# A fused convolution and SiLU block: 25 weight sums spread over GpSimd's queue, and one block's halo moved ahead of another's stores

## The chip, the cores and the metric

The kernel runs on one core of a Trainium2 chip. The metric is the device time of one execution in microseconds (us). Before the change it is 2310.44 us, the median of three runs (2310.09 to 2311.41).

The engines are named TensorE (PE in the profile, its weight loads PEld), VectorE (DVE), ScalarE (ACT), GpSimd (POOL) and SyncE (SP). Each runs its own instructions in the order of the program and waits at semaphores for the others. SyncE does nothing but issue DMAs; GpSimd issues the DMAs that add to their destination.

## The reference

```python
# x: (8, 4096, 192), weight: (8 heads, 7 taps), w_in: (192, 2048), w_out: (2048, 192)
w = exp(weight - max(weight)); w = w / (sum(w) + 1e-9)      # per head
x_pad = concat(zeros(6 rows), x)                            # along the sequence
y[b, s, h, :] = sum_k w[h, k] * x_pad[b, s + k, h, :]       # 24 channels per head
h = y.reshape(32768, 192) @ w_in
out = (h * sigmoid(h)) @ w_out
```

So each token's 192 channels are first replaced by a weighted sum over seven tokens, and then go through two matrix products with a SiLU between them.

## The kernel before

**Tiling.** The 32768 tokens are taken in 32 blocks of 1024 (`TT`), and a block is held as two halves of 512 on the two halves of the 128 partitions. The 192 channels are three groups of 64. The hidden layer's 2048 columns are 16 chunks of 128.

**A block's stages.** `ld` loads the block into the tile `nat` by SyncE (L167). `i.2`, `i.1`, `i.0` are VectorE transposes of its three channel groups into `xt` (`turn_in`, L502). `xt` is one tile for all blocks, and a block has one of two `nat` tiles. `ha.0` (`halo_in`, L514) puts the six tokens before each half into the head of `xt`: for the first half a copy of a saved tail (by ScalarE for the blocks up to the fourth, L521), for the second half a DMA from the first half's end by SyncE (L524). `v.ki` is tap `i` of channel group `k` (`conv`, L530). Its first tap is a ScalarE product that writes into `nat` (L539). From the third block's group 2 on, each later tap is a ScalarE product into a buffer called `u` (L542) and a DMA of GpSimd that adds this to `nat` (L543); before that, VectorE adds the taps (L547). `sp` copies the result into the tile `dup` by SyncE (L569) and `w` makes differences of it on VectorE (`win`).

**The products.** Both matrix products are done with fewer multiplications, in the manner of Strassen: 15 products `P` for each of five groups of blocks of `w_in` (`P5.1` is product 5 of group 1, L681), three plain ones `L`, and 20 products `Q` for each quarter of `w_out` (L817). The results of the `P` products are combined on ScalarE and VectorE: a token `u4.1` is a ScalarE copy of a partial result into a `u` buffer (L730), `X`, `a` and `b` are VectorE sums (L724), `S` and `SL` the SiLU on ScalarE (L742, L747). There are ten `u` buffers for these copies and for the taps together. They are a list from whose front a buffer is taken and to whose end it is returned, in the order of the program; a tap's buffer goes back to the list at once, so that its next user has to wait for the tap's DMA. Sums of the SiLU's results are `tA1` (GpSimd), `tB1`, `tC`, `tD` and `t5` to `t13` (VectorE, all L806).

**The weights' own sums.** The products need sums of weight blocks, and GpSimd makes them in place, once: for `w_in` in `combine` (the `late` ones of these in steps `go`), for `w_out` in `combine_out` (L449), which runs through the 25 sums of `OUT_SUMS`, each of 128x256 numbers into `wall` or `wx` (recorded at L149, the helper that pins the order). The first block does its second product without those sums (`down_plain`, L889, steps `dp`) from the plain `w_out`, so that the 25 sums must come behind its last reading of `wall`, and ahead of the second block's `Q` products.

**The order.** Everything stands in an order written out by hand. `START` (L106) holds the steps from the first block to the second, `PLAN` (L80) one pass that is run again for each later block, `FINISH` the end. A sign ahead of a token tells whose it is: none is the pass's own block, `-` the block before, `=` the one before that, `+` the next one. `step` (L939) does a token once; what `START` has done, the passes leave out. `START` is read as of the third block, so that `+i.2` in it is of the fourth, `-P5.4` of the second and `=dp.0` of the first. Before the change, all 25 sums are emitted inside the last `dp` step of `START`. The fourth block's `i.1` stands at the end of the pass in which the second block's own products begin, and its `i.2`, `i.0` and `ha.0` at the beginning of the next, thus behind `=stp.0 =stp.1 =stp.2`, the twelve stores of the first block (L930), which wait for its output transposes `op` on VectorE (L921) and the copies `cp` on ScalarE (L913).

In the pass that is changed, the second block's products run in this order (the first twelve are `P5.4 P5.0 P2.4 P2.0 P3.4 P6.4 P6.0 P3.0 P1.0 P1.4 P13.4 P9.4`), with some of the steps of other engines between them:

```text
P5.1 u0.0 P13.0 P0.0 S2.4 u0.4 +v.20 P0.4 P9.0 P12.4 X4.4 u5.1 S2.0 P11.4 u1.4 P2.1 P7.4
... +v.10 ... P4.4 b5.4 a1.4 S3.0 +v.11 P3.1 ... P5.2 S0.4 S2.1 P10.0 P2.3 u5.2 u4.3 +v.00
... tA1 P7.1 ... P12.3 P0.3 +v.12 P9.2 a5.3 tC2 P0.2 P13.2 P4.3 S4.3 +v.24 ... P8.2 Q4.3 ...
```

Of the kernel before, what the change touches and what calls it, by code (L numbers as in the profile page):

```python
# [17 lines left out]
def kernel(  # L18
# [33 lines left out]
    NK = D // R  # L52
# [7 lines left out]
    NJ = NM // 2  # L60
# [56 lines left out]
    )  # L117
    FINISH = (
# [22 lines left out]
    def pin(ins):  # L141
        return tc.keep_in_program_order(ins)
# [110 lines left out]
    def load_in(j, queue, ks=None):  # L253

        if ("i", j) not in raws:
            raw_tile(("i", j))
        raw = raws["i", j].rearrange(AS[j], a=2, k=NK)
        for e in range(2) if ks is None else ():
            for a in range(2):
                queue.dma_start(  # L260
                    out=raw[R * e : R * e + R, a, :, :], in_=in32[:, :, a, 2 * j + e, :]
                )
        for k in ks or ():
            for e in range(2):
                queue.dma_start(
                    out=raw[R * e : R * e + R, :, k, :], in_=in32[:, k, :, 2 * j + e, :]
                )
# [77 lines left out]
    def comb(out, u, v, op):  # L345
        pool.tensor_tensor(out, u, v, op=op)
# [3 lines left out]
    def raw(g, i, k, e):  # L350
        a, j, own = chunks(g)[i]
        return rows(wr[j] if own == e else ws[j], e)[:, a, k, :]

    def combine(g, e):
# [38 lines left out]
    OUT_SUMS = (  # L393
        (("o", 7), ("o", 4), "+", ("o", 7)),
        (("x", 0), ("o", 1), "+", ("o", 7)),
        (("o", 1), ("o", 1), "+", ("o", 4)),
        (("o", 4), ("o", 4), "+", ("o", 10)),
        (("x", 1), ("o", 11), "+", ("o", 4)),
        (("o", 4), ("o", 4), "n", ("o", 4)),
        (("x", 2), ("o", 5), "+", ("x", 1)),  # L400
        (("x", 1), ("o", 8), "-", ("x", 1)),
# [41 lines left out]
    def out_form(at):  # L443
        if at[0] == "x":
            return wx[:, at[1], :, :]
        k, third = divmod(at[1], NK)
        return wall[:, :, k // 2, k % 2, R * third : R * third + R]

    def combine_out():  # L449
        for to, u, sign, v in OUT_SUMS:  # L450
            u = zeros[:, 0:R].unsqueeze(1).to_broadcast([P, NJ, R]) if sign == "n" else out_form(u)
            comb(out_form(to), u, out_form(v), ALU.add if sign == "+" else ALU.subtract)

    load_in(0, nc.sync, (0,))

# [149 lines left out]
    def rows(t, e):  # L605
        return t[R * e : R * e + R]
# [48 lines left out]
    def chain_bank(b, g, c):  # L655
        return banks[CHAIN_BANKS[c][g]]

    def x_bank(b, g, o):
        return banks[XBANKS[o][g]]
# [4 lines left out]
    def columns(half):  # L664
        return slice(0, TB) if half is None else slice(half * TB // 2, (half + 1) * TB // 2)

    def product(b, g, r, half=None):
        cols = columns(half)
        e = int(r in ON_B and (g, r) != SWAP)
        if r in RIGHT:  # L670
            rhs = rows(wins[b], e)[:, RIGHT[r], :]
        else:
            rhs = rows(dups[b], e)[:, SLOT[e][X_OF[r]], :]
        if r in (13, 11):
            to, first = x_bank(b, g, 2 if r == 13 else 4), False
        else:
            c = next(c for c in range(3) if r in CHAINS[c])
            to, first = chain_bank(b, g, c), r == CHAINS[c][0] and (b, g, c) not in begun
            begun.add((b, g, c))
        pin(  # L680
            nc.tensor.matmul(  # L681
                to[:, cols],
                raw(g, *LEFT[e][r], e),
                rhs[:, cols],
                start=first,
                stop=True,
                skip_group_check=True,
            )
        )
# [101 lines left out]
    def g_part(name, js):  # L791
        kind, i = name[0], int(name[1:])
        if kind == "s":
            return g_part(G_SUMS[i][3], js)
        if kind == "t":
            return temps[i][:, js, :]
        k, n = divmod(i, 2)
        at = TB * (2 * n + k % 2)
        return gall[:, js, k // 2, at : at + TB]
# [8 lines left out]
    def out_bank(node):  # L808
        name, e = OUT_HOME[node]
        return rows(banks[OUT_BANKS[name]], e)  # L810

    def out_product(b, r, j):
        node = next(x for x in OUT_ORDER if r in OUT_ORDER[x])
        first = node in ("X", "Y", "O4") and (b, node) not in begun
        begun.add((b, node))
        pin(
            nc.tensor.matmul(  # L817
                out_bank(node),
                out_form(OUT_FORMS[r])[:, j, :],
                g_part(OPERAND[r], j),  # L820
                start=first,
                stop=True,
                skip_group_check=True,
            )
        )
# [46 lines left out]
    def turn_out(b, i):  # L872
        pin(nc.vector.transpose(mid(2 + i), mid(i - 1)))  # L873
# [15 lines left out]
    def down_plain(b):  # L889

        cmbs[b] = [xpool.tile([P, 4, TB], F32, tag="cmb", name="cmb")]
        for j in range(NJ):
            for a in range(2):
                for e in range(2):
                    for k in range(NK):
                        for n in range(2):
                            pin(
                                nc.tensor.matmul(  # L898
                                    banks[DOWN_BANKS[k]][R * n : R * n + R, :],
                                    wo[j][:, a, e, R * k : R * k + R],  # L900
                                    g_tile(b, j, a)[:, n, e, :],
                                    start=j == 0 and a == 0 and e == 0,
                                    stop=j == NJ - 1 and a == 1 and e == 1,
                                    skip_group_check=True,
                                )
                            )
                        if (a, e, k) == (1, 1, NK - 1):
                            if j == NJ - 1:
                                combine_out()
                        yield  # L910

    def copy_plain(b, k):
# [26 lines left out]
    def step(b, token):  # L939

        if token[0] in BACK:
            b, token = b - BACK[token[0]], token[1:]
        name, _, arg = token.partition(".")
        if b < 0 or b >= NB or (b, token) in did:
            return
        did.add((b, token))
        digits = [int(c) for c in arg] if arg.isdigit() else []
        if name[0] == "P":
            product(b, digits[0], int(name[1:]))
        elif name == "L":  # L950
            plain(b, *digits)
        elif name == "SL":
            silu_plain(b, *digits)
        elif name[0] in "uXabS":
            sums_h(b, name, *digits)
        elif name[0] == "Q":
            out_product(b, int(name[1:]), *digits)
        elif name[:2] == "tA":
            sum_g(b, int(name[2:]), slice(0, NJ - 1), nc.gpsimd)
        elif name[:2] == "tB":  # L960
            sum_g(b, int(name[2:]), slice(NJ - 1, NJ), nc.vector)
        elif name[:2] in ("tC", "tD"):
            i = NJ // 2 if name[1] == "D" else 0
            sum_g(b, int(name[2:]), slice(i, i + NJ // 2), nc.vector)
        elif name[0] == "t":
            sum_g(b, int(name[1:]), slice(0, NJ), nc.vector)
        elif name in ("O", "C", "d"):
            out_copy(b, token)
        elif name == "m":
            out_sum(b, *digits)  # L970
        elif name == "o":
            turn_out(b, *digits)
        elif name == "st":
            store_out(b, *digits)
        elif name == "dp":
            next(downs)
        elif name == "cp":
            copy_plain(b, *digits)
        elif name == "op":
            turn_plain(b, *digits)  # L980
        elif name == "stp":
            store_plain(b, *digits)
        elif name == "go":
            some(late, digits[0])
        elif name == "ld":
            load(b, digits)
        else:
            {"i": turn_in, "ha": halo_in, "v": conv, "sp": spread, "w": win}[name](
                b, *digits
            )  # L990
# [62 lines left out]
    def some(ups, n):  # L1053
        for _ in range(n):
            next(ups, None)
# [71 lines left out]
```

## Time and profile before

| | us |
|---|---|
| median of three runs | 2310.44 |
| lowest and highest | 2310.09, 2311.41 |
| the profiled execution | 2310.77 |
| its span, first to last instruction | 2309.1 |
| idle before ScalarE's `u` copies (L730), whole span | 125.2 |
| GpSimd busy | 655.7 |
| one pass of 1024 tokens, for example from 225.07 to 295.42 | 70.35 |

The mean granted clock of TensorE is 0.998 of full speed over the span.

How to read what follows: times are from the span's start. A row of a timeline has start, duration, engine, line, operation, what it writes and reads, and in brackets how long the engine was idle before it and what ended that. A row of the waits has who waited for whom, the total, how many times, and the longest. A row of a line has the shortest, median and longest duration in ns. "To landing" is the time from a DMA's issue until its semaphore tells of its completion.

### The profile page before, as it was taken

Reading aid. Unit: us, or ns where it says so; the run is one execution under the profiler, and the core shown is the slowest. Engines: PE = TensorE matmul, PEld = TensorE weight load, DVE = VectorE, ACT = ScalarE, POOL = GpSimd, SP = SyncE. Lnnn points to the kernel's source line nnn. Section 1 sums busy time; section 2 is a strip of 40 time slices with the busy share of each in tenths; the row PEclk is TensorE's granted clock in tenths of the full one; section 3 lists DMA queues with packets and bytes.
Section 4 is the critical chain, followed back from the end, with each engine's and each line's share of the span. In section 5 each row is a group of like instructions: output and inputs, shape, how many; then the busy total and the mean of one; then the engine's idle time right before and its main releaser. Section 6 shows DMA issues by size and latency. Waiting matters only on the chain.

```text
span 2309.1 us, 31726 instructions
## 1 busy us (share of the span) xinstructions
PE 2290.7 (99%) x10622; PEld 926.5 (40%) x10622; DVE 2004.6 (87%) x2265; ACT 1554.1 (67%) x2842; POOL 655.7 (28%) x734
## 2 busy tenths in 40 slices
PE   9989999999999999999999999999999999999998
PEld 4334333444333444334443334443345433344433
DVE  8768888988889888889888898888898889888887
ACT  6367666776667776667766677766677766677543
POOL 5752223222223222232222232222332222322200
PEclk9999999999999999999999999999999999999999
DMA  7544577665677655676656676556765566765411
GB/s 167 103 88 87 99 124 128 108 105 99 109 121 126 105 100 96 121 129 112 105 99 108 117 131 104 103 95 117 127 119 103 97 105 117 130 108 96 74 32 19
DMA packets 527139, 244.22 MB, mean 106 GB/s; under 512 B 431936, under 2 KB 437056, under 8 KB 526976
## 3 DMA queue, kind: packets, MB, share of 16 engines
q0 software_dynamic: 76480, 140.02, 35.7%
q1 hardware_dynamic: 446272, 101.65, 24.8%
q8 instruction: 84, 1.38, 0.2%
q10 hardware_dynamic: 4224, 0.52, 0.2%
q14 instruction: 79, 0.65, 0.1%
HBM read 31.46 MB, written 25.17 MB: 25 GB/s over the span
## 4 chain that ended last, share of the span: by engine, by line
PE 99%; DMA 0%; POOL 0%; ACT 0%; DVE 0%; issue 0%; SPq 0%; ACTq 0%
PE ps L817 47%; PE ps L681 45%; PE ps L698 3%; PE ps L898 2%; PE ps L622 2%; PE ps L1005 1%; PE ps L460 0%; DMA nat<-u 0%; DMA dup<-nat 0%; DMA nat<-in_x_dram 0%; ACT u L730 0%; POOL wall L149 0%; POOL wx L149 0%; DVE yx L873 0%; DVE cmb L865 0%
## 5 line engine op out<-in xcount | busy, mean ns | idle before, releaser
L543 POOL DMA_DIRECT2D nat<-u x528 | 452.6, 930 | 1246.9 <-ACT u L542 822.2
L817 PE MATMUL ps<-g,wall 128*64 128x512 f32 x1984 | 743.7, 595 | 0.0
L681 PE MATMUL ps<-win,wr 64*128 64x512 f32 x1550 | 685.9, 599 | 10.6 <-ACT u L730 10.6
L681 PE MATMUL ps<-win,ws 64*128 64x512 f32 x1550 | 645.0, 592 | 0.4 <-ACT u L730 0.4
L730 ACT COPY u<-ps 128x512 f32<-128x512 f32 x775 | 439.5, 590 | 125.2 <-issue 58.9
L817 PE MATMUL ps<-g,wx 128*64 128x512 f32 x1240 | 415.2, 592 | 0.0
L681 PE MATMUL ps<-dup,wr 64*128 64x512 f32 x868 | 401.6, 590 | 0.0
L817 PE MATMUL ps<-t,wall 128*64 128x512 f32 x992 | 369.1, 594 | 0.0
L542 ACT ACTIVATE u<-xt,taps 128x512 f32<-128x512 f32 x528 | 357.7, 716 | 0.7
L681 PEld LDWEIGHTS ps<-win,wr 64*128 64x128 f32 x1550 | 256.5, 187 | 226.4 <-issue 129.4
L724 DVE TENSOR_TENSOR g<-u,ps 128x512 f32<-128x512 f32 x465 | 309.5, 682 | 32.9 <-PE ps L681 30.6
L681 PEld LDWEIGHTS ps<-win,ws 64*128 64x128 f32 x1550 | 257.1, 187 | 121.8 <-issue 96.2
L817 PEld LDWEIGHTS ps<-g,wall 128*64 128x64 f32 x1984 | 215.8, 137 | 222.1 <-issue 212.9
L742 ACT ACTIVATE g<-g 128x512 f32<-128x512 f32 x465 | 280.9, 631 | 34.1 <-DVE g L724 34.1
L742 ACT ACTIVATE g<-ps 128x512 f32<-128x512 f32 x465 | 279.9, 602 | 28.9 <-PE ps L681 28.2
L724 DVE TENSOR_TENSOR ps<-u,ps 128x512 f32<-128x512 f32 x310 | 214.9, 693 | 94.9 <-ACT u L730 32.6
L681 PE MATMUL ps<-dup,ws 64*128 64x512 f32 x682 | 269.7, 590 | 0.0
L817 PE MATMUL ps<-t,wx 128*64 128x512 f32 x744 | 267.3, 594 | 0.0
L806 DVE TENSOR_TENSOR t<-g 128x512 f32<-128x512 f32 (+1 forms) x186 | 241.2, 1311 | 4.3
L852 ACT COPY cmb<-ps 64x512 f32<-64x512 f32 x124 | 72.1, 581 | 236.4 <-PE ps L817 210.6
L806 DVE TENSOR_TENSOR t<-g,t 128x2048 f32<-128x2048 f32 x93 | 212.9, 2289 | 8.3 <-PE ps L817 7.1
L817 PEld LDWEIGHTS ps<-g,wx 128*64 128x64 f32 x1240 | 129.5, 137 | 211.1 <-issue 210.2
(103 smaller groups left out, 2474.3 us busy)
## 6 DMA issues: line engine op xcount, KB each, us to landing
nat<-u POOLq DMA_DIRECT2D x528, 256.0 KB, 4.2
dup<-nat SPq DMA_DIRECT2D x345, 128.0 KB, 2.4
nat<-in_x_dram SPq DMA_DIRECT2D x382, 64.0 KB, 3.9
out_dram<-yx SPq DMA_DIRECT2D x244, 64.0 KB, 2.1
out_dram<-cmb SPq DMA_DIRECT2D x122, 64.0 KB, 4.4
raw<-in_moe_w_out_dram SPq DMA_DIRECT2D x8, 384.0 KB, 4.2
g<-in_moe_w_in_dram SPq DMA_DIRECT2D x8, 192.0 KB, 5.5
ws<-wr POOLq DMA_DIRECT2D x8, 192.0 KB, 5.0
```

Source lines behind the costliest of these rows:

```text
L542: pin(nc.scalar.activation(z, src, AF.Copy, scale=tap))
L543: pin(nc.gpsimd.dma_start(out=dst, in_=z, accum_op=ALU.add))
L622: nc.tensor.matmul(hs[a, n, e], rows(wr[j], e)[:, a, k, :], rows(d, e)[:, n, k, :], start=k == 0, stop=k == NK - 1,)
L681: nc.tensor.matmul(to[:, cols], raw(g, *LEFT[e][r], e), rhs[:, cols], start=first, stop=True, skip_group_check=True,)
L698: nc.tensor.matmul(plain_bank(b, n and 1 + e)[:, cols], rows(wr[j] if own == e else ws[j], e)[:, a, k, :], rows(dups[b], e)[:, SLOT[e][2 * ...
L724: pin(nc.vector.tensor_tensor(out_, u, v, op=op))
L730: pin(nc.scalar.copy(us[b, g, o][:, cols], t1[:, cols]))
L742: pin(nc.scalar.activation(h, src, AF.Silu))
L806: pin(engine.tensor_tensor(g_part(to, js), g_part(u, js), g_part(v, js), op=op))
L817: nc.tensor.matmul(out_bank(node), out_form(OUT_FORMS[r])[:, j, :], g_part(OPERAND[r], j), start=first, stop=True, skip_group_check=True,)
L852: pin(nc.scalar.copy(to(), out_bank(node)))
L898: nc.tensor.matmul(banks[DOWN_BANKS[k]][R * n : R * n + R, :], wo[j][:, a, e, R * k : R * k + R], g_tile(b, j, a)[:, n, e, :], start=j == ...
```

## The change

It has two parts. `combine_out` becomes a generator that stops after each sum. The second block's products are counted as they are emitted, and from the 13th on each odd one is followed by one sum; whatever is left is emitted ahead of the first `Q` product. In `START`, the fourth block's three transposes are put among the third block's last taps, and its `ha.0` ahead of the first block's stores.

```diff
-        "v.12 v.13 v.14 v.15 v.16 v.04 v.05 v.06 =dp.45 =cp.0 -P2.4 -P2.0 -L.01 -u4.0 -u4.4 "
-        "=dp.46 =dp.47 =cp.1 =cp.2 =op.0 =op.1 =op.2 =stp.0 =stp.1 =stp.2"
+        "v.12 v.13 v.14 v.15 v.16 v.04 +i.2 v.05 +i.1 v.06 +i.0 =dp.45 =cp.0 -P2.4 -P2.0 -L.01 "
+        "-u4.0 -u4.4 =dp.46 =dp.47 =cp.1 =cp.2 =op.0 =op.1 =op.2 +ha.0 =stp.0 =stp.1 =stp.2"
...
             comb(out_form(to), u, out_form(v), ALU.add if sign == "+" else ALU.subtract)
+            yield
+
+    out_sums, first_ps = combine_out(), []
...
-                        if (a, e, k) == (1, 1, NK - 1):
-                            if j == NJ - 1:
-                                combine_out()
                         yield
...
             product(b, digits[0], int(name[1:]))
+            if b == 1:
+                first_ps.append(token)
+                if len(first_ps) > 12 and len(first_ps) % 2:
+                    some(out_sums, 1)
...
         elif name[0] == "Q":
+            some(out_sums, len(OUT_SUMS))
             out_product(b, int(name[1:]), *digits)
```

`some(ups, n)` takes the next `n` steps of a generator. `comb` is a GpSimd `tensor_tensor` held in program order.

## The prediction

> **What bounds the kernel now.** I read the page first, then who TensorE waited for, then its timeline where those waits lie, and last the three queues that end them.
>
> ```profile
> span 2309.1 us, 31726 instructions
> PE 2290.7 (99%) x10622; PEld 926.5 (40%) x10622; DVE 2004.6 (87%) x2265; ACT 1554.1 (67%) x2842; POOL 655.7 (28%) x734
> PE ps L681 <- ACT u L730: 11.0, 3, 8.5
> 109.32 1.12 PE L681 MATMUL ps<-win,ws 64*128 64x512 f32 x2 [0.40 <-ACT u L730]
> 117.26 0.69 PE L681 MATMUL ps<-win,wr 64*128 64x512 f32 x1 [2.11 <-ACT u L730]
> 128.28 0.59 PE L681 MATMUL ps<-win,ws 64*128 64x512 f32 x1
> 137.39 2.08 PE L681 MATMUL ps<-win,wr 64*128 64x512 f32 x4 [8.53 <-ACT u L730]
> ```
>
> TensorE is the bound, 99% busy. Of its 18.4 us of idle time, 11.0 lie in three waits between 109 and 138 us, among the second block's first products, and all three end on ScalarE's copy to `u` (L730). The next view, busy time by stretches, sets this stage beside the same products one pass later (duration; then busy time of TensorE, weight loads, VectorE, ScalarE, GpSimd; granted clock; DMA share; GB/s).
>
> ```profile
> 109.32:154.73 45.41, 34.77 (x152) 18.47 (x154) 23.99 (x36) 27.64 (x53) 26.84 (x34) 0.92 0.37 68
> 193.29:225.00 31.71, 31.71 (x154) 15.56 (x152) 27.35 (x42) 27.10 (x52) 6.09 (x4) 1.00 0.32 63
> 137.39:141.00 3.61, 3.61 (x10) 1.66 (x12) 0.69 (x1) 2.17 (x5) 1.46 (x1) 0.59 0.00 0
> ```
>
> From P1 of group 0 to the first output product the second block takes 45.41 us, the third 31.71. **13.70 us is the most that this stage can give back.** It holds more than the waits: after the long one the granted clock is 0.59 for 3.61 us. The reasons for the waits stand in the timelines of ScalarE, GpSimd and the DMA queue of SyncE:
>
> ```profile
> 116.02 0.72 ACT L539 ACTIVATE nat<-xt,taps 128x512 f32<-128x512 f32 x1 [3.19 <-DMA dup<-nat]
> 116.64 0.56 ACT L730 COPY u<-ps 128x512 f32<-128x512 f32 x1
> 120.59 0.77 ACT L542 ACTIVATE u<-xt,taps 128x512 f32<-128x512 f32 x1
> 126.86 0.60 ACT L742 ACTIVATE g<-ps 128x512 f32<-128x512 f32 x1 [0.28 <-PE ps L681]
> 136.76 1.07 ACT L730 COPY u<-ps 128x512 f32<-128x512 f32 x2 [9.30 <-DMA nat<-u]
> 113.78 0.45 POOL L149 TENSOR_TENSOR ws<-ws,wr 64x128 f32<-64x128 f32 x1
> 114.31 0.72 POOL L149 TENSOR_TENSOR wall<-wall 128x256 f32<-128x256 f32 x1
> 132.78 0.72 POOL L149 TENSOR_TENSOR wx<-zeros,wx 128x256 f32<-128x256 f32 x1
> 133.45 0.82 POOL L543 DMA_DIRECT2D nat<-u  x1
> 103.78 8.44 SPq L930 DMA_DIRECT2D out_dram<-osb  x12
> 112.33 0.60 SPq L524 DMA_DIRECT2D xt<-xt  x1
> 113.03 14.62 SPq L569 DMA_DIRECT2D dup<-nat  x4
> ```
>
> **The long wait.** ScalarE writes a tap product of the fourth block (`v.11`) into a `u` buffer at 120.59. GpSimd is to add it to `nat` by DMA, but its queue holds all 25 output sums without a gap from 114.31, so that the DMA is issued at 133.45. There are ten `u` buffers, taken in turn; counting the takes and returns in the program, the next to take this one is `u5.2`, the copy at 136.76. P2 of group 2 needs that copy, and TensorE stands 8.53 us.
>
> **The middle wait.** `v.20`, the fourth block's first tap (L539), stops ScalarE for 3.19 us; the copy behind it, at 116.64, is what TensorE waits for. The view names a copy to `dup`, which `v.20` neither reads nor overwrites. What it does read is the halo, issued at 112.33 behind twelve stores:
>
> ```profile
> DMA to landing us min/median/max: 3.4/3.4/3.4
> ```
>
> So the halo (the only L524 of 104 to 140 us) landed at 115.7, 0.3 before `v.20` began.
>
> **The change, part by part.**
>
> *Sums spread.* They keep number, order and form; only GpSimd's program order changes, since no sum waits for a product. One follows each odd product from the 13th on. By the plan's tokens that gives 8 sums ahead of `v.11`'s DMA, 9 more ahead of GpSimd's part of an input sum (`tA1`, L806), 7 ahead of `v.12`'s DMA, and the last ahead of `v.24`'s. One sum costs (133.45 - 114.31) / 25 = 0.766 us. The 13th product is P5 of group 1, before `v.20`; no sum can start before 114.3, as the queue is busy until then with the sums at 113.78. So `v.11`'s DMA goes at 114.31 + 8 x 0.766 = 120.4 instead of 133.45. For what must be in time I use the third block's pass, counted from its first output product at 225.00:
>
> ```profile
> 211.07 3.54 POOL L806 TENSOR_TENSOR t<-g 128x1536 f32<-128x1536 f32 x1 [8.21 <-ACT g L742]
> 208.24 1.07 ACT L730 COPY u<-ps 128x512 f32<-128x512 f32 x2
> 227.31 1.06 ACT L730 COPY u<-ps 128x512 f32<-128x512 f32 x2
> 228.59 0.69 PE L681 MATMUL ps<-win,wr 64*128 64x512 f32 x1
> DMA to landing us min/median/max: 3.2/4.2/7.2
> ```
>
> (The last is L543's between 130 and 240 us.) If the stage ends 12.2 us earlier, the first output product is at 154.73 - 12.2 = 142.5. `u5.2` (208.24) is then due at 125.8; its buffer is free at 120.4 + 4.2 = 124.6. In time by 1.2; with the longest landing late by 1.8. `tA1` (211.07) is due at 128.6; the 17th sum ends at 120.4 + 0.85 + 9 x 0.766 = 128.1. In time. Behind `tA1`: 128.6 + 3.54 + 7 x 0.766 = 137.5 for `v.12`, then 0.85 and one sum, and `v.24` goes at 139.1. Its buffer is the next to serve `u5.0` of the third block, the copy at 227.31, due at 144.8; it lands at 143.3, in time by 1.5, late by 1.5 with the longest landing. That copy has little slack: the products at 228.59 follow its pair by 0.2 us. The sums end at 139.1, 3.4 us before the first output product reads one.
>
> So the 8.53 us go, and with them the slow clock: 3.61 x (1 - 0.59) = 1.48 us.
>
> The Trainium skill ("TensorE: Matmul & The Clock Gate", Part 1) says that the clock halves after about 3.4 us of idleness and comes back after about 3.4 us of work, 1.7 us lost by an estimate from that page. The row has 1.48, and the sum would be 0.2 larger by the page.
>
> *Halo ahead.* Three transposes move up VectorE's queue, ahead of the last taps of the third block and the first block's output transposes; the copy of the halo's other half moves up ScalarE's queue past `SL.0`, and L524 up SyncE's queue past the twelve stores.
>
> ```profile
> 100.74 0.75 DVE L547 SCALAR_TENSOR_TENSOR nat<-xt,taps,ps 128x512 f32<-128x512 f32 x1
> 103.04 0.71 DVE L921 STREAM_TRANSPOSE osb<-cmb 128x512 f32<-128x512 f32 x1 [1.56 <-ACT cmb L913]
> 107.45 1.86 DVE L502 STREAM_TRANSPOSE xt<-nat 128x512 f32<-128x512 f32 x3
> 106.20 0.58 ACT L913 COPY cmb<-ps 128x512 f32<-128x512 f32 x1 [0.27 <-PE ps L898]
> 108.10 0.60 ACT L747 ACTIVATE g<-ps 128x512 f32<-128x512 f32 x1 [1.31 <-PE ps L681]
> 108.59 0.19 ACT L521 COPY xt<-tail 64x18 f32<-64x18 f32 x1
> 86.50 7.18 SPq L167 DMA_DIRECT2D nat<-in_x_dram  x12
> ```
>
> VectorE's taps end at 101.5; with 1.86 more the transposes end at 103.4, inside its idle 1.56 but for 0.3 by which the first output transpose slips. Their input was issued by 93.7 and, with the 7.2 of the slowest transfer above, lands by 100.9; only then would they stop the engine, and for under a microsecond. The halo is issued at 103.4 and lands at 106.8; `v.20` wants it at 112.8 (116.02 - 3.19). The copy at 108.59 goes into the 1.31 us that ScalarE idles before 108.10. Behind L524 the stores slip by 0.3 + 0.6; the transfers at 113.03 come next, and the products that follow do not use what these bring (the third block does), so that this is free. If that cover were gone it would be 0.9. The 2.11 us go: ScalarE's copy at 116.64 moves to 113.4, ends at 114.0, and TensorE wants it at 117.26 - 2.11 = 115.15. Of the 0.40 at 109.32, the 0.10 that the halo copy took (108.59 until the next copy) goes; the rest stays, since it is the wait for `SL.0`.
>
> **Sum:** 8.53 + 1.48 + 2.11 + 0.10 = 12.2 us. Nothing after 154.73 shows a TensorE wait, so the gain keeps to the end. The profiled execution took 2310.77 us (span 2309.1), 0.33 over the median 2310.44; less 12.2 that is 2298.6, or **2298.2** by the median. The unexplained 13.70 - 12.2 = 1.5 is pairing and small waits that may go too.
>
> **A rule against it.** Two rows show what a sum costs beside VectorE:
>
> ```profile
> L149 POOL TENSOR_TENSOR wall<-wall x12: 721/728/1187, 114.3 to 131.4; 128x256 f32<-128x256 f32 x12
> 126.74 1.87 POOL L149 TENSOR_TENSOR wall<-wall 128x256 f32<-128x256 f32 x2
> 126.93 1.09 DVE L806 TENSOR_TENSOR t<-g 128x512 f32<-128x512 f32 x1
> 207.51 0.68 DVE L806 TENSOR_TENSOR t<-g 128x512 f32<-128x512 f32 x1
> ```
>
> The one VectorE add of two SBUF operands amid the sums took 1.09 instead of 0.68 us, and the dearest sum, 1.187 instead of 0.728, is of that time (two in 1.87 us at 126.74). The spread sums meet one such add more, `tC2`: 0.46 on GpSimd, 0.4 to 0.8 on VectorE, inside the margin of 1.5 above. The Trainium skill ("GPSIMD Engine Reference", Key points) says the two engines share SBUF interfaces and contend when VectorE reads two SBUF inputs; the trace agrees (1.09 against 0.68), and were every sum so met, the last rival below would follow.
>
> **Rivals.**
> 1. *A smaller wait takes the place of the one removed*: 17 sums still stand ahead of `v.12`'s and `v.24`'s DMAs. With the longest landings and the dear sums, 1.5 to 4 us are lost again at `u5.2` or `u5.0`: 2299.7 to 2302.2. For: 0.2 us of slack at 228.59. Against: median landing leaves 1.2 and 1.5.
> 2. *The halo is not what `v.20` waited for*; the copy to `dup` is, or another wait keeps ScalarE. Then 10.0 us go: 2300.4. Against: the landing at 115.7.
> 3. *The change does not do what it says*: the sums still run in one stretch ahead of `v.11`, or another order moves. 2310.4. Against: each follows a token that I can count.
> 4. *Slower*: the sums run dear in their new place. At c us each, `v.24` is issued at 114.31 + 25c + 0.85 + 3.54 + 0.85 and lands at 123.75 + 25c; every microsecond past 144.8 is TensorE's. It eats the whole gain at c = 1.33; at 1.6 the wait is 19.0, and the time 2310.4 - 12.2 + 19.0 = 2317.2. Against: one row of 25 comes to 1.187.
>
> **How the numbers follow.** The forecast 0.67, rival 1 0.18, rival 2 0.06, rival 3 (or a like wait in full) 0.05, rival 4 0.04. Under 0.2% (4.6 us) a measurement of this kernel cannot tell from no change. Faster: 0.67 + 0.18 + 0.06 = 0.91; same 0.05; slower 0.04. The range goes from the whole 13.70 (2296.7) to the far end of rival 1 (2302.2).
>
> **What would show it.** TensorE has no wait over 0.5 us between 109 and 155; the stretch to the first output product is 32 to 33.5 us; the clock stays at 1.00; L524 is issued near 103.5, and L539 starts near 112.8; `v.11`'s DMA near 120.4; `tA1` no later than 129. A wait of `u` L730 on the DMA `nat<-u` near 125 or 144 makes rival 1; a ScalarE wait at L539 rival 2. I am wrong altogether if TensorE waits in later passes, which now have none.

## The result and the profile after

| | before, us | after, us |
|---|---|---|
| median | 2310.40 (2310.09 to 2311.41, 4 runs) | 2298.49 (2297.91 to 2299.04, 4 runs) |
| the profiled execution | 2310.77 | 2298.43 |
| its span | 2309.1 | 2296.4 |

The ratio is 0.9948, with a 95% interval of 0.993 to 0.9965. The gain is 11.9 us by the medians and 12.3 in the profiled executions. The forecast was 2298.2.

In the changed kernel the lines between L453 and L905 have moved by three: the products are L684, the `u` copies L733, a first tap L542, a later tap L545, GpSimd's DMA L546, the halo L527, `sp` L572, `w` L589, the input sums L809, the output products L820, the plain ones L701. The stores stay at L930.

First the engines' line of the page, then the row of TensorE's waits for `u` in the whole span (total, times, longest):

```profile
PE 2288.8 (100%) x10622; PEld 930.8 (41%) x10622; DVE 2004.8 (87%) x2265; ACT 1554.2 (68%) x2842; POOL 656.2 (29%) x734
```

```profile
PE ps L684 <- ACT u L733: 0.3, 1, 0.3
```

Of the 11.0 us of waits for `u`, 0.3 are left. The same stretches as before, in four pieces at whose borders the same products stand, and the pass behind them (duration; busy time of TensorE, weight loads, VectorE, ScalarE, GpSimd; granted clock; DMA share; GB/s), first of the kernel before, then of the changed one:

```profile
109.32:113.84 4.52, 4.52 (x18) 2.57 (x20) 1.99 (x3) 2.08 (x4) 2.27 (x5) 1.00 0.94 140
113.84:126.99 13.15, 11.04 (x57) 6.95 (x55) 6.50 (x11) 9.81 (x20) 12.13 (x18) 1.00 0.24 44
126.99:141.51 14.52, 5.99 (x22) 2.62 (x19) 3.60 (x6) 3.78 (x8) 9.17 (x11) 0.76 0.26 45
141.51:154.73 13.22, 13.22 (x64) 6.33 (x62) 11.90 (x18) 11.96 (x23) 3.27 (x3) 1.00 0.44 91
154.73:225.07 70.34, 70.34 (x330) 28.19 (x332) 61.40 (x69) 49.24 (x91) 19.08 (x20) 1.00 0.56 100
```

```profile
109.18:113.71 4.53, 4.53 (x18) 2.55 (x20) 1.99 (x3) 3.11 (x7) 3.30 (x6) 1.00 1.01 146
113.71:124.20 10.49, 10.49 (x58) 8.03 (x56) 7.08 (x11) 8.95 (x19) 9.78 (x15) 1.00 0.35 72
124.20:128.06 3.86, 3.86 (x21) 2.60 (x18) 2.97 (x5) 3.57 (x8) 3.70 (x5) 1.00 0.50 89
128.06:141.28 13.22, 13.22 (x64) 8.57 (x62) 11.90 (x18) 11.94 (x24) 11.13 (x11) 1.00 0.37 70
141.28:212.49 71.21, 71.21 (x330) 28.54 (x332) 61.49 (x69) 49.38 (x91) 19.08 (x20) 1.00 0.58 103
```

The second piece, with the middle wait, lost 2.66 us. The third, with the long wait and the half clock, lost 10.66. The first and the fourth are as they were. So the stretch went from 45.41 to 32.10, by 13.31. But the pass behind it has grown by 0.87, at the same number of matmuls. The stretch begins 0.14 earlier and the rest of the span differs by 0.12; together 12.7, the difference of the spans.

The pass's 0.87 stand in one place. Here are VectorE's first step of `w` and the products about it in the timelines of the changed kernel, and then the same products before:

```profile
144.13 0.69 DVE L589 TENSOR_TENSOR win<-dup 128x512 f32<-128x512 f32 x1 [0.99 <-DMA dup<-nat]
...
144.79 1.12 PE L701 MATMUL ps<-dup,ws 64*128 64x512 f32 x2
145.69 0.67 PE L684 MATMUL ps<-win,wr 64*128 64x512 f32 x1
...
147.58 0.64 PE L820 MATMUL ps<-t,wx 128*64 128x512 f32 x1
```

```profile
158.24 0.69 PE L698 MATMUL ps<-dup,ws 64*128 64x512 f32 x1
158.25 0.69 PE L681 MATMUL ps<-win,wr 64*128 64x512 f32 x1
...
160.16 0.64 PE L817 MATMUL ps<-t,wx 128*64 128x512 f32 x1
```

Before, the plain product (L698) and the first Strassen product of the third block (L681) start together. After, `w.0` waits 0.99 us for a copy to `dup`, the plain product runs alone, and the other follows 0.90 later. From the plain product to the next output product it is 1.92 us before and 2.79 after: the 0.87. No wait of TensorE tells of it, since some matmul was always running.

The queues that the prediction spoke of, in the changed kernel: GpSimd, ScalarE, VectorE's `tC2` and SyncE's DMA queue:

```profile
113.08 0.73 POOL L149 TENSOR_TENSOR wall<-wall 128x256 f32<-128x256 f32 x1
119.33 0.85 POOL L546 DMA_DIRECT2D nat<-u  x1
127.45 3.53 POOL L809 TENSOR_TENSOR t<-g 128x1536 f32<-128x1536 f32 x1
133.80 1.71 POOL L149 TENSOR_TENSOR wall<-zeros,wall 128x256 f32<-128x256 f32 x1
136.83 0.86 POOL L546 DMA_DIRECT2D nat<-u  x1
138.12 1.16 POOL L546 DMA_DIRECT2D nat<-u  x1
...
112.58 0.73 ACT L542 ACTIVATE nat<-xt,taps 128x512 f32<-128x512 f32 x1
124.57 1.07 ACT L733 COPY u<-ps 128x512 f32<-128x512 f32 x2
143.65 1.08 ACT L733 COPY u<-ps 128x512 f32<-128x512 f32 x2
...
133.68 1.25 DVE L809 TENSOR_TENSOR g<-g,t 128x1024 f32<-128x1024 f32 x1
...
103.17 0.60 SPq L527 DMA_DIRECT2D xt<-xt  x1
135.23 7.18 SPq L572 DMA_DIRECT2D dup<-nat  x7
```

`v.11`'s DMA goes at 119.33 instead of 133.45, the halo at 103.17 instead of 112.33, and neither `v.20` (112.58) nor `u5.2` (124.57) nor `u5.0` (143.65) shows idle time ahead of it. The two late DMAs, `v.12`'s and `v.24`'s (136.83, 138.12), are issued while SyncE issues the seven copies to `dup`.

### The profile page after: what moved, and what is told of

The parts are those of the page before. It is cut to its first block, busy times and chain, and to the rows that moved or that the text cites. A ratio compares the mean times of both kernels' runs of the same rounds, so it can differ in the third digit from the quotient of the medians.

```text
span 2296.4 us, 31730 instructions
## 1 busy us (share of the span) xinstructions
PE 2288.8 (100%) x10622; PEld 930.8 (41%) x10622; DVE 2004.8 (87%) x2265; ACT 1554.2 (68%) x2842; POOL 656.2 (29%) x734
## 4 chain that ended last, share of the span: by engine, by line
PE 100%; DVE 0%; issue 0%; ACT 0%; ACTq 0%
PE ps L820 47%; PE ps L684 45%; PE ps L701 3%; PE ps L901 2%; PE ps L625 2%; PE ps L1010 1%; PE ps L463 0%; DVE yx L876 0%; DVE cmb L868 0%; ACT u L733 0%; PE ps L489 0%; DVE zeros L149 0%; DVE warm L149 0%; ACTq L733 0%; ACT g L750 0%
## 5 line engine op out<-in xcount | busy, mean ns | idle before, releaser
L546 POOL DMA_DIRECT2D nat<-u x528 | 453.0, 930 | 1238.6 <-ACT u L545 798.8
L820 PE MATMUL ps<-g,wall 128*64 128x512 f32 x1984 | 743.8, 596 | 0.0
L684 PE MATMUL ps<-win,wr 64*128 64x512 f32 x1550 | 684.7, 598 | 0.0
L684 PE MATMUL ps<-win,ws 64*128 64x512 f32 x1550 | 644.1, 592 | 0.3 <-ACT u L733 0.3
L733 ACT COPY u<-ps 128x512 f32<-128x512 f32 x775 | 439.5, 590 | 114.7 <-issue 58.9
L820 PE MATMUL ps<-g,wx 128*64 128x512 f32 x1240 | 415.2, 593 | 0.0
L684 PE MATMUL ps<-dup,wr 64*128 64x512 f32 x868 | 401.4, 590 | 0.0
L820 PE MATMUL ps<-t,wall 128*64 128x512 f32 x992 | 369.2, 594 | 0.0
L545 ACT ACTIVATE u<-xt,taps 128x512 f32<-128x512 f32 x528 | 357.7, 716 | 0.7
L684 PEld LDWEIGHTS ps<-win,wr 64*128 64x128 f32 x1550 | 256.8, 186 | 215.3 <-issue 129.1
L727 DVE TENSOR_TENSOR g<-u,ps 128x512 f32<-128x512 f32 x465 | 309.5, 682 | 32.1 <-PE ps L684 29.9
L820 PEld LDWEIGHTS ps<-g,wall 128*64 128x64 f32 x1984 | 216.0, 137 | 222.3 <-issue 213.0
L684 PEld LDWEIGHTS ps<-win,ws 64*128 64x128 f32 x1550 | 257.3, 187 | 119.4 <-issue 92.2
L684 PE MATMUL ps<-dup,ws 64*128 64x512 f32 x682 | 270.1, 590 | 0.0
L820 PE MATMUL ps<-t,wx 128*64 128x512 f32 x744 | 267.3, 595 | 0.0
L809 DVE TENSOR_TENSOR t<-g 128x512 f32<-128x512 f32 (+1 forms) x186 | 240.9, 1309 | 4.3
L809 DVE TENSOR_TENSOR t<-g,t 128x2048 f32<-128x2048 f32 x93 | 212.9, 2289 | 8.0 <-PE ps L820 6.8
L820 PEld LDWEIGHTS ps<-g,wx 128*64 128x64 f32 x1240 | 129.6, 137 | 211.0 <-issue 210.1
```

What stands on the lines that cost most here:

```text
L545: pin(nc.scalar.activation(z, src, AF.Copy, scale=tap))
L546: pin(nc.gpsimd.dma_start(out=dst, in_=z, accum_op=ALU.add))
L684: nc.tensor.matmul(to[:, cols], raw(g, *LEFT[e][r], e), rhs[:, cols], start=first, stop=True, skip_group_check=True,)
L727: pin(nc.vector.tensor_tensor(out_, u, v, op=op))
L733: pin(nc.scalar.copy(us[b, g, o][:, cols], t1[:, cols]))
L809: pin(engine.tensor_tensor(g_part(to, js), g_part(u, js), g_part(v, js), op=op))
```

## The experiments

Each was timed beside the kernel before on the same chip, the first four on one (before: 2310.07) and the others on another (before: 2309.91). The diffs are against the changed kernel.

| | median, us | ratio to before, 95% |
|---|---|---|
| e1_again, the changed kernel | 2298.33 | 0.9950 (0.9937 to 0.9962) |
| e1_halo_alone | 2309.77 | 1.0001 (0.9993 to 1.0010) |
| e1_sums_alone | 2300.23 | 0.9960 (0.9946 to 0.9974) |
| e1_last4_later | 2297.70 | 0.9947 (0.9934 to 0.9959) |
| e2_changed, the changed kernel | 2297.76 | 0.9949 (0.9936 to 0.9961) |
| e2_last4_again, as e1_last4_later | 2297.58 | 0.9946 (0.9933 to 0.9960) |
| e2_after_v11 | 2307.81 | 0.9991 (0.9982 to 1.0000) |
| e2_no_sums | 2299.88 | 0.9956 (0.9943 to 0.9970) |

**The two parts one by one.** The theory was that the halo's 2.11 and the sums' 10.0 are two separate waits. The rivals: that they share, so that one part alone brings less or nothing, and that the halo is not what `v.20` waits for.

The changed kernel once more, as the yardstick on the same chip:

> The changed kernel once more, beside the others. All theories: 2298.5 us within 0.7, first output product near 141.3 us from the span's start, and the pass from there to the next first output product 71.2 us instead of the 70.35 of the passes before and after it.

It took 2298.33, and its two stretches were 32.11 and 71.13: both the gain and the loss behind it come back.

The halo alone, with the sums in one stretch as before:

```diff
-            yield
...
+                        if (a, e, k) == (1, 1, NK - 1):
+                            if j == NJ - 1:
+                                combine_out()
...
-                if len(first_ps) > 12 and len(first_ps) % 2:
-                    some(out_sums, 1)
```

> Only the order in START is changed; the 25 sums run in one stretch as before. Theory (the middle wait is the halo's, the long one is GpSimd's queue): L539 of the fourth block no longer waits and starts near 112.6, but the sums still hold the tap's DMA until they are done. They can start at 113.1 instead of 114.3 us, as in the changed kernel, so the DMA goes at 132.2 and only 1.2 us are gained: 2309.2 us, first output product near 153.5, the long wait longer than before (about 9.5 us). Rival, gains add up: 2.2 us, 2308.2. Rival, the copy to dup is what L539 waited for: its 3.2 us wait stays, gain near 0.

Measured: 2309.77 over 11 runs (2308.80 to 2312.43), nothing that can be told from no change. The timelines of ScalarE, GpSimd and TensorE, then three pieces right behind the long wait, in this kernel's profiled execution (lines as before the change):

```profile
111.74 0.73 ACT L539 ACTIVATE nat<-xt,taps 128x512 f32<-128x512 f32 x1
131.38 0.82 POOL L543 DMA_DIRECT2D nat<-u  x1
135.32 2.08 PE L681 MATMUL ps<-win,wr 64*128 64x512 f32 x4 [10.40 <-ACT u L730]
```

```profile
135.32:138.00 2.68, 2.68 (x6) 1.19 (x8) 0.48 (x1) 2.06 (x4) 0.53 (x1) 0.50 0.00 0
138.00:141.00 3.00, 3.00 (x10) 1.37 (x8) 1.02 (x3) 1.23 (x3) 2.98 (x1) 0.50 0.00 0
141.00:144.00 3.00, 3.00 (x14) 1.15 (x12) 1.96 (x3) 2.63 (x6) 0.00 (x0) 0.93 0.00 0
```

`v.20` waits for nothing, so the halo did what it should. But TensorE now stands from 124.92 (135.32 - 10.40) instead of 128.86 (137.39 - 8.53), 3.94 earlier, while the DMA that ends the wait goes only 2.07 earlier (131.38 instead of 133.45), since the sums ahead of it wait for no product. (About 1 us of both is an earlier start: in this execution P1 of group 0 stands at 108.34 and not at 109.32.) So the long wait is longer by the difference, 1.87. Behind it the clock stays at 0.50 for two of these pieces, some 5.7 us, and the loss by the clock is 2.68 x 0.50 + 3.00 x 0.50 + 3.00 x 0.07 = 3.05 us, against 1.48 before. In this execution the longer wait and the longer half clock took more than the middle wait gave: the stretch is 45.89 us, against 45.41 before, and the time 2310.80, one us over the median of the eleven. The theory had the mechanism, but expected a wait of about 9.5 us and 1.2 us of gain. By the interval, 2308.2, where the gains add up, is just excluded, and 2309.2 is not.

The sums alone, with the halo behind the stores as before (`START` is that of the kernel before):

```diff
-        "v.12 ... v.04 +i.2 v.05 +i.1 v.06 +i.0 ... =op.2 +ha.0 =stp.0 =stp.1 =stp.2"
+        "v.12 ... v.04 v.05 v.06 ... =op.2 =stp.0 =stp.1 =stp.2"
```

> Only the sums are spread; START as before. Theory: the long wait and the slow clock go, the 3.2 us wait of L539 for the halo stays with a TensorE wait of about 2.1 us: 2300.7 us (2.2 slower than the changed kernel), first output product near 143.5. Rival, the halo's part is worthless once GpSimd is free: 2298.5.

Measured: 2300.23, 1.90 over the changed kernel. The timelines of ScalarE and SyncE, and the stretch:

```profile
115.27 0.72 ACT L542 ACTIVATE nat<-xt,taps 128x512 f32<-128x512 f32 x1 [2.69 <-DMA xt<-xt]
...
111.70 0.84 SPq L527 DMA_DIRECT2D xt<-xt  x1
```

```profile
109.08:143.81 34.73, 33.12 (x152) 20.57 (x154) 23.95 (x36) 27.53 (x53) 27.80 (x34) 1.00 0.46 79
```

Here the view itself names the halo (`xt<-xt`) ahead of `v.20`, where before it named a copy to `dup`, and TensorE stands 1.61 us. The stretch is 2.63 longer than in the changed kernel, close to the 2.66 that its second piece lost; the pass behind it takes 70.61, which is 0.5 to 0.6 less than in the changed kernel (71.13, 71.21), so that less than 2.63 shows in the time. By the medians the halo is worth 0.3 us or nothing without the spread sums and 1.9 with them, and the sums alone 9.8: the parts do not add up. The intervals are wider than the 1.6 that are missing; what shows the cause is the long wait in the trace of e1_halo_alone.

**Why the next pass lost 0.87.** Theory: `v.12`'s and `v.24`'s DMAs are so late that they hold up the copies to `dup`, for which `w.0` waits. Rivals: the copies come late because TensorE frees their places later in relation to them, or the sums themselves, beside VectorE, are what costs. The same 25 sums, but the last four behind the two DMAs:

```diff
-                if len(first_ps) > 12 and len(first_ps) % 2:
+                n = len(first_ps)
+                if n % 2 and (12 < n < 54 or n > 64):
                     some(out_sums, 1)
```

> The changed kernel, but the last four sums are emitted behind v.24 instead of ahead of v.12 and v.24 (after products 65, 67, 69 and 71). Theory: the changed kernel loses 0.87 us in the pass that begins with the first output product, because the DMAs of v.12 and v.24 go 2.8 and 2.9 us late behind the sums and run beside the copies to dup that the first difference (w.0) of the third block waits for. Here v.12 goes near 134.0 and v.24 near 135.1, w.0 has no wait, that pass takes 70.4 us, and the time is 2297.6. Rival, the copies to dup are late only because TensorE frees their places later in relation to them: the pass stays at 71.2 and the time at 2298.5.

Measured: 2297.70, 0.63 under the changed kernel. GpSimd's and VectorE's timelines and the stretches of the profiled execution:

```profile
134.32 0.88 POOL L546 DMA_DIRECT2D nat<-u  x1
135.42 0.84 POOL L546 DMA_DIRECT2D nat<-u  x1 [0.22 <-issue]
...
143.33 0.69 DVE L589 TENSOR_TENSOR win<-dup 128x512 f32<-128x512 f32 x1
```

```profile
108.53:141.55 33.02, 32.96 (x152) 20.07 (x154) 24.18 (x36) 27.69 (x53) 27.04 (x34) 1.00 0.51 94
141.55:211.90 70.35, 70.35 (x330) 28.18 (x332) 61.42 (x69) 49.24 (x91) 19.11 (x20) 1.00 0.56 100
```

The DMAs go 2.5 and 2.7 us earlier, `w.0` waits for nothing and the pass is 70.35 again. The first stretch is 0.9 longer in this execution: `u1.4`'s copy (L733, at 114.64) stands 1.01 us behind a tap's DMA of the third block, which the change does not touch. Another run of the same kernel, with the changed one beside it:

> The kernel with the last four sums later once more, beside the changed kernel. Theory: 0.6 to 0.9 us under the changed kernel, 2297.6, with a pass of 70.4 us behind the first output product. Rival: no difference from 2298.4.

> The changed kernel, to stand beside the others of this call: 2298.4 us, a pass of 71.1 to 71.2 us behind the first output product.

Of e2_last4_again and then of e2_changed, the two stretches:

```profile
109.10:141.19 32.09, 32.09 (x152) 21.70 (x154) 23.85 (x36) 27.56 (x53) 27.11 (x34) 1.00 0.51 93
141.19:211.54 70.35, 70.35 (x331) 28.17 (x332) 61.43 (x69) 49.33 (x91) 19.11 (x20) 1.00 0.56 100
```

```profile
108.34:140.44 32.10, 32.10 (x152) 21.32 (x154) 24.27 (x36) 27.56 (x53) 27.96 (x34) 1.00 0.46 83
140.44:211.42 70.98, 70.98 (x330) 28.63 (x332) 61.51 (x69) 49.33 (x91) 19.07 (x20) 1.00 0.58 103
```

The stretch is the same, 32.1, and the pass 70.35 against 70.98 (71.13 and 71.21 in the two other profiled executions of the changed kernel). So the loss goes with the place of the two DMAs. Where the stretch is 32.1 with and without the loss, TensorE does not free the places at another time; and in e1_last4_later the last four sums run beside the copies (from 135.98 on) without a loss. The size follows too: `v.12`'s DMA goes 1.60 us behind the first copy in the changed kernel (0.87 lost), 1.34 behind it in e1_sums_alone (70.61, so 0.26 lost), and 1.08 ahead of it in e1_last4_later (none). By the medians the difference is 0.63 on the first chip and 0.18 on the second, both inside the spread of the runs; the stretch itself begins anywhere from 108.3 to 109.3 in executions of one kernel, more than the gain. That this version beats the changed kernel is seen in the traces and not settled by the times.

**How late the sums may be.** The prediction took `u5.2` and `u5.0` for what is late first. If so, all 25 sums right behind `v.11`'s DMA should cost a few us. They are emitted there and nowhere else:

```diff
-                if len(first_ps) > 12 and len(first_ps) % 2:
-                    some(out_sums, 1)
...
+            if (b, token) == (3, "v.11"):
+                some(out_sums, len(OUT_SUMS))
```

> The changed kernel, but all 25 sums are emitted in one stretch right behind v.11's DMA, none between products. It tells the spreading itself from the one DMA that it lets through. Theory (each DMA of a tap has a due time, the one of the next user of its buffer, and only lateness past it costs): v.11's DMA goes near 118.2 and u5.2 is not held up, but tA1 starts near 138 instead of 127.5, v.12's DMA goes near 141.5 and v.24's near 142.6 and they land near 145.3 and 147.5; v.04 (due 141.4) and u5.0 (due 143.6) then wait about 4 us, and TensorE with them: 2301 to 2302 us, with a TensorE wait or a stretch of slow products between 141 and 149. Rival, only v.11's DMA matters: 2298.4 or, as w.0 is free of the late DMAs, 2297.6.

Measured: 2307.81, ten us over the changed kernel, so that size and place of the expectation were wrong. GpSimd's, VectorE's and TensorE's timelines and the stretch:

```profile
118.31 0.85 POOL L546 DMA_DIRECT2D nat<-u  x1 [5.02 <-PE ps L684]
138.37 3.42 POOL L809 TENSOR_TENSOR t<-g 128x1536 f32<-128x1536 f32 x1
...
141.82 1.23 DVE L809 TENSOR_TENSOR g<-g,t 128x1024 f32<-128x1024 f32 x1 [8.26 <-POOL t L809]
...
143.71 1.22 PE L684 MATMUL ps<-win,wr 64*128 64x512 f32 x1 [7.03 <-DVE ps L727]
```

```profile
108.53:151.64 43.11, 36.08 (x152) 20.77 (x154) 24.05 (x36) 28.59 (x55) 26.71 (x34) 0.88 0.40 72
```

`v.11` is in time, but now GpSimd's input sum `tA1` starts at 138.37 instead of 127.45. `tC2` on VectorE needs it, stands 8.26 us, and holds up the sums of `P` results queued behind it, for which TensorE waits 7.03. The stretch is 11.0 longer than in the changed kernel: 7.03, and 3.98 of busy time, of which at least 2.15 go to the clock (0.50 over the 4.29 us behind the wait, from 143.71 to 148.00). The pass behind the stretch takes 70.34.

**What the sums cost at all.** All 25 are left out, and `wx` is only zeroed, once at the start, so that the output products read other weights than the reference has:

```diff
+    pool.memset(wx, 0.0)
...
-                if len(first_ps) > 12 and len(first_ps) % 2:
-                    some(out_sums, 1)
...
-            some(out_sums, len(OUT_SUMS))
```

> The changed kernel with all 25 sums of the output weights left out (the Q products read the plain weights and zeros), so that its output is not the reference's. It shows what the sums still cost in the changed kernel. Theory: only the 0.87 us at w.0, as in the kernel with the last four sums later: 2297.6 us, the stretch to the first output product 32.1 us, the pass behind it 70.4. Rival, the sums also slow the products' stretch (VectorE or the weight reads beside GpSimd): that stretch comes to the 31.7 us of later passes, 2297.2.

Measured: 2299.88, which misleads: with the zeroing (1.80 us on GpSimd, at 3.39) the whole program is later, and P1 of group 0 starts at 111.40 instead of 108.3 to 109.3. The stretches tell more:

```profile
111.40:143.58 32.18, 32.18 (x152) 17.77 (x154) 23.88 (x36) 27.67 (x53) 8.77 (x9) 1.00 0.51 95
143.58:213.93 70.35, 70.35 (x331) 28.17 (x332) 61.43 (x69) 49.23 (x91) 19.10 (x20) 1.00 0.56 100
```

Without any sum the stretch is 32.18, no shorter than with 25 of them (32.10), so the rival falls. In their new place they cost TensorE nothing there, and nothing is left to gain from them but the 0.6 to 0.9 of the pass behind.

## Why the prediction was right, and where it was not

- **The long wait** was right in cause and due time. `v.11`'s DMA was forecast at 120.4 and went at 119.33, eight sums behind the first, which started 1.2 earlier (113.08) than the prediction allowed. That start varies from execution to execution: the tap's DMA of the third block that stands ahead of them goes 2.10 us behind P1 of group 0 in the kernel before, 0.99 in the changed one, 0.63 in e2_changed, the same kernel, and 2.03 in e1_last4_later. `u5.2` found its buffer free. Right too: the halo at 103.5 (103.17), `v.20` at 112.8 (112.58), `tA1` by 128.6 (127.45), the clock at 1.00, no wait over 0.5 us.
- **The middle wait**: the halo was its cause, and e1_sums_alone shows it, since there the view names it. In the kernel before, the first of the copies issued from 113.03 on landed 3.4 us after its issue, at 116.4, and `v.20` had started at 116.02; so it cannot have waited for them. Rival 2 falls.
- **The clock** was right as a mechanism; its size is no constant (1.5 us in the profile before, 3.05 in e1_halo_alone, at least 2.15 in e2_after_v11).
- **The 0.10** at 109.32 came (0.40 to 0.30), but the start of the stretch varies by ten times as much from execution to execution.
- **The sum left out two terms that nearly cancel.** The terms in the stretch make 12.12, and it gave 13.31. The prediction saw the other 1.2 as "pairing and small waits that may go too", in the range and not in the sum. By the pieces above, 2.66 - 2.11 = 0.55 lie around the middle wait and 10.66 - 10.01 = 0.65 around the long one. In part they are pairing, since TensorE counts as busy while one product runs alone: the last matmul ahead of the middle wait (114.56) starts 0.29 after its neighbour and the last ahead of the long one (128.28) 0.33, and each ends alone. How much of the 1.2 this is, no run shows. The other way, 0.87 were lost in the next pass at `w.0`. That the prediction did not have: it held that "the gain keeps to the end". That the forecast came within 0.3 us is luck: the two nearly balance.
- **Rival 1**, a smaller wait in place of the one removed, came in kind but at another place: not at `u5.2` or `u5.0`, but where VectorE waits for the copies to `dup`, behind the two late DMAs. `v.24`'s landing at 143.55 (issued at 138.12, 5.4 later) left `u5.0`, which started at 143.65, no slack to speak of; the forecast margin of 1.5 was gone, because the products came 1.2 earlier than forecast.
- **Rival 4 followed one path only.** It let dear sums cost time where `v.24` lands after `u5.0` is due; by its own formula that begins at (144.8 - 123.75) / 25 = 0.84 us for each sum, and at 1.33 the gain is gone. e2_after_v11 shows a second path, by `tA1`: `tC2` starts at 133.68 in the changed kernel, and `tA1` ends at 127.45 + 3.53 = 130.98, so 2.7 us are left there, or 0.16 more for each of the 17 sums ahead of it. The price of a dear sum was low as well: the dearest took 1.71 us (at 133.80, beside `tC2`), where the prediction's dearest row was 1.187. VectorE's side was cheap: that `tC2` took 1.25, against 1.23 in e2_after_v11, where no sum ran beside it.
- **The parts were priced as if they stood alone.** 2.11 and 10.0 are right only together: with the long wait in place, what the halo gives cannot be told from nothing (0.3 us by the medians).

Still open is by what the late DMAs slow the copies to `dup`. How long the copies take from issue to landing is known; here are the last two of the seven, in the changed kernel and then in the one before:

```profile
DMA to landing us min/median/max: 4.1/4.2/4.3
```

```profile
DMA to landing us min/median/max: 2.2/2.3/2.4
```

With the first two of the seven it is the other way about: 2.2 and 2.4 in the changed kernel, 3.3 and 4.4 before. So copies are slowed before too, but other ones, those that are under way beside the two DMAs; before, these are the first, and `w.0` has no wait. In e1_last4_later it is as in the kernel before, in e1_again as in the changed one. That the DMAs' place decides is shown. That they share DMA engines or a memory's ports is only argued; no run took the two apart.

## What to carry to other kernels

One-off work on an engine that runs in order is placed by what stands behind it in that queue: list for each later transfer and each later operand when its reader wants it, and cut the work there; the first to be late may be an operand for another engine's queue (`tA1`, which `tC2` reads) and not the transfer one was looking at. Two waits in a row are not two gains: if the second is ended by a queue that goes its own way, what is taken from the first only makes the second longer, until that queue is mended too. A TensorE that is "busy" may be running one of two products that belong side by side; compare the same products' time across passes, not the waits alone.

## What the runs showed of the hardware

- **The half clock behind a wait lasts unequally long, and the longer wait need not have the longer one.** After 8.53 us of idleness the clock was 0.59 over 3.61 us; after 10.40 us (e1_halo_alone) it was 0.50 over 5.68 us and a little less than full behind that; after 7.03 us (e2_after_v11) it was 0.50 over 4.29 us. The price was 1.5, 3.05 and at least 2.15 us. The Trainium skill ("TensorE: Matmul & The Clock Gate", Part 1) says that the window by which the clock is judged runs freely, so that the time of the return varies from run to run. The three durations agree with that, but each is one execution of another kernel, so none shows the chance itself; its 3.4 us for the return are exceeded by the 4.29 and the 5.68.
- **A GpSimd sum and a VectorE sum of two SBUF operands are dearer side by side, and either may pay.** A GpSimd sum of 0.73 us became 1.71 beside `tC2`, whose own time was 1.25 instead of 1.23. In the kernel before both paid: 0.46 us on GpSimd at 126.74, and 1.09 instead of 0.68 on VectorE at 126.93.
